# Two long fp32 dummy matmuls in place of the first bf16 ones, and a K pair split 2 to 6 around the second scale sums

## The chip, the cores and the metric

The kernel runs on one core of one Trainium2 chip. The metric is device time in microseconds (us) of one execution. The kernel before had a median of 244.20 us in three runs (244.18 to 244.32).

## The reference, cut to what matters

One block of a diffusion transformer: modulation from `c`, attention, MLP. Only its first lines touch this change.

```python
mod = (_silu(c) @ w_mod).reshape(B, 6, 1, D)              # B=2, D=1152
shift_a, scale_a, gate_a, shift_m, scale_m, gate_m = [mod[:, i] for i in range(6)]
h = _layernorm(x, axis=-1) * (1 + scale_a) + shift_a      # x: 2 x 256 x 1152
qkv = (h @ wqkv).reshape(B, N, 3, H, Dh)
# ... attention, output projection, second LayerNorm, MLP
```

## The kernel before: the parts that matter here

The program is a list of "units" per engine, and the waits follow from tracked reads and writes. TensorE takes its units in program order. Every instruction raises its engine's counter by one, and whoever depends on it waits for a value of that counter:

```python
for ins in u.instrs:
    ...
    bi = ins.fn(eng_handle)
    if ins.dma_sem is not None:
        bi.then_inc(dma_sems[ins.dma_sem], 16)
    else:
        bi.then_inc(sems[e], 1)
```

Some names. The "scale sums" are SiLU(c) times the scale columns of `w_mod`, made in matmuls only 2 columns wide (one per batch element). Their weights come in two sets of columns, each in three transfers ("pieces") of three row blocks. "K" is the K third of `qkv`, whose weights come one row block at a time. HBM is the chip's memory, from which the weights are loaded.

The start. Dummy matmuls are meant to bring TensorE to full clock before the needed work comes; their results are thrown away. (The code here is cut, and its comments are added.)

```python
# Pool: ones, identity (IDENT), ...
dve(270, lambda e: e.memset(Q4B, 0.0), [], [Q4B], "zq4b")
for i in range(5):
    S.unit("pe", 430.0, "warm_a%d" % i)
    mm(ps32(5), IDENT, Q4B, True, True)            # 128x512 bf16 dummy
# then c is transposed (c_T), and SiLU(c) is made on ScalarE and VectorE
# ...
warm(7, "b")                                       # seven more dummies
for n, behind in ((1, "bn_ln1_1_1"), (1, "aggr_ln1_1"), (2, "veps_ln1_1"), (2, "rstd_ln1_1")):
    warm(n, behind, behind)                        # dummies behind LayerNorm's steps
xn_T(1)                                            # first needed work: transposes
sca(0, 3)                                          # scale sums, first third of the weights
warm(1, "d")
sca(3, 6)                                          # second third
warm(1, "f", "aggr_ln1_2")
xn_T(0)
sca(6, 9)                                          # last third
xn_T(2, 0, 8)
# ...
k_first(0)                                         # first K matmuls
```

The second scale sums (the other five of nine column blocks, each `mod_kt` five matmuls 2 columns wide), with a K pair of eight 256-column matmuls around their last third:

```python
def k12(part):
    kts = ((range(3), ()), (range(3, KC), range(KC)))[part]     # KC = 4: 3 matmuls, then 5
    ...
for kt in range(KT):                               # KT = 9
    if kt == 6:
        k12(0)
    mod_kt(WSC, kt, 0, "scb_%d" % kt, (KC, KT))
hk(KC, 0)                                          # VectorE: first tile scaled by these sums
# ...
k12(1)
# then the K matmuls that read the scaled tiles
```

## Time and profile before

| | before |
|---|---|
| time, median of three | 244.20 us |
| span of the profiled run (243.62 us as a whole) | 242.3 us |
| TensorE busy | 238.4 us (98%) |
| needed work begins on TensorE | 7.98 us |
| first K matmul | 11.184 us |
| bubble at the second scale sums | 123 ns |

A row of the timeline has start, length, engine, line, what is written and read, the number of instructions, and in brackets how long the engine was idle before and what ended it. PEld is TensorE's weight load, which starts with its matmul or ahead of it, so its bracket shows what a matmul waited for. Beside what the views print, the trace holds a record of every rise of a semaphore: those of the transfers ("landings") and those of TensorE's counter. Numbers with three decimals here are from these records and from the start of each instruction.

### The profile page before, as it was taken

To read this page: it belongs to the slowest core of one execution; us is meant where nothing else is said; L and a number is where in the kernel's file an instruction comes from. 1 tells how busy PE (TensorE), PEld (TensorE's weight loads), DVE (VectorE), ACT (ScalarE), POOL (GpSimd) and SP (SyncE) were. 2 spreads that over 40 slices of the span, in tenths; PEclk is the share of its full clock that TensorE was granted. 3 is DMA by queue.
4 is the path that set the end of the run, shared out by engine and by line. 5 is a ranking of instruction groups with operands and counts; after the bars stand their busy time and mean duration, and the time that the engine had idled before them with its cause. 6 is when DMAs were issued, how large, how long until landed. Compare 5 with 4: busy or idle time off the path is not lost.

```text
span 242.3 us, 4076 instructions
## 1 busy us (share of the span) xinstructions
PE 238.4 (98%) x1763; PEld 147.5 (61%) x1763; DVE 120.3 (50%) x218; ACT 67.0 (28%) x136; POOL 21.2 (9%) x39
## 2 busy tenths in 40 slices
PE   7999999999999999999999999999999999999996
PEld 2698854556667666898444444444566656656676
DVE  3814388696997699789999500000022222111112
ACT  5820350355424107973233322222000000000000
POOL 1400000000021186400000000020000000000000
PEclk9999999999999999999999999999999999999999
DMA  6999999999996999989953498012000000000001
GB/s 241 330 381 392 391 392 391 397 413 405 391 356 196 351 395 391 391 266 394 314 164 82 150 320 313 0 29 72 0 16 19 16 16 19 16 16 16 19 24 27
DMA packets 30140, 51.59 MB, mean 213 GB/s; under 512 B 1703, under 2 KB 15787, under 8 KB 30123
## 3 DMA queue, kind: packets, MB, share of 16 engines
q1 hardware_dynamic: 29680, 50.14, 58.0%
q0 software_dynamic: 416, 1.19, 1.6%
q8 instruction: 14, 0.23, 0.4%
q14 instruction: 3, 0.02, 0.0%
q10 hardware_dynamic: 27, 0.00, 0.0%
HBM read 50.14 MB, written 1.19 MB: 212 GB/s over the span
## 4 chain that ended last, share of the span: by engine, by line
PE 97%; DVE 2%; POOL 0%; issue 0%; ACT 0%; DVEq 0%; POOLq 0%
PE psum L688 95%; PE psum L691 2%; DVE arena L739 1%; DVE arena L760 0%; POOL arena L711 0%; DVE arena L740 0%; DVE arena L1284 0%; DVE arena L1285 0%; POOL arena L710 0%; ACT arena L726 0%; DVE arena L727 0%; DVE arena L732 0%; DVE arena L742 0%; POOL arena L717 0%; POOL arena L715 0%
## 5 line engine op out<-in xcount | busy, mean ns | idle before, releaser
L688 PE MATMUL psum<-arena 128*128 128x384 bf16 (+10 forms) x1674 | 234.9, 306 | 1.6 <-POOL arena L711 1.5
L688 PEld LDWEIGHTS psum<-arena 128*128 128x128 bf16 (+3 forms) x1674 | 142.3, 97 | 90.0 <-issue 3.8
L1079 DVE SCALAR_TENSOR_TENSOR arena<-arena 128x1152 f32<-128x1152 bf16 x32 | 44.7, 1414 | 0.6
L1284 DVE TENSOR_TENSOR arena<-psum,arena 128x384 f32<-128x384 f32 (+3 forms) x14 | 7.0, 501 | 68.0 <-PE psum L688 68.0
L1193 ACT ACTIVATE arena<-psum 128x512 bf16<-128x512 f32 (+1 forms) x44 | 22.4, 520 | 42.7 <-PE psum L688 42.7
L683 ACT ACTIVATE arena<-psum 128x512 bf16<-128x512 f32 (+6 forms) x37 | 19.6, 549 | 39.5 <-PE psum L688 37.1
L685 DVE CAST arena<-psum 128x512 bf16<-128x512 f32 (+3 forms) x13 | 8.2, 641 | 11.4 <-PE psum L688 11.3
L669 POOL DMA_DIRECT2D dit_scratch<-arena x3 | 1.8, 616 | 115.7 <-DVE arena L685 58.9
L1161 POOL TENSOR_TENSOR arena<-arena 128x384 f32<-128x384 f32 x12 | 10.9, 910 | 10.8 <-DVE arena L1160 9.5
L1106 DVE CAST arena<-psum 72x32 bf16<-72x32 f32 x1 | 0.2, 186 | 21.3 <-PE psum L688 21.3
L739 DVE BATCH_NORM_STATS2 arena<-arena 128x6 f32<-128x384 f32 (+1 forms) x18 | 9.5, 552 | 0.1
L1166 ACT ACTIVATE arena<-arena 128x1152 bf16<-128x1152 f32 x4 | 5.3, 1345 | 11.9 <-DVE arena L1165 11.9
L691 PEld LDWEIGHTS psum<-arena 128*128 128x128 bf16 (+1 forms) x89 | 5.8, 98 | 2.5 <-issue 0.8
L1160 DVE TENSOR_TENSOR arena<-psum,arena 128x384 f32<-128x384 f32 x12 | 6.5, 549 | 1.6 <-DMA arena<-dit_scratch 1.6
L1285 DVE TENSOR_TENSOR arena<-arena 128x384 bf16<-128x384 f32 (+3 forms) x14 | 7.0, 501 | 0.5
L691 PE MATMUL psum<-arena 128*128 128x128 bf16 (+1 forms) x89 | 7.1, 219 | 0.1
L1180 DVE TENSOR_SCALAR arena<-psum,arena 128x128 bf16<-128x128 bf16 x20 | 5.4, 341 | 1.9 <-PE psum L691 1.9
L1183 ACT ACTIVATE arena<-psum,arena 128x128 bf16<-128x128 bf16 x16 | 6.0, 456 | 0.9 <-PE psum L688 0.6
L1086 DVE TENSOR_REDUCE arena<-arena 128x36 f32<-128x1152 f32 x4 | 5.4, 1348 | 0.0
L1083 DVE STREAM_TRANSPOSE arena<-arena 128x1152 f32<-128x1152 f32 x4 | 5.4, 1364 | 0.0
L1009 ACT ACTIVATE arena<-psum,arena 128x256 bf16<-128x256 f32 x8 | 3.7, 472 | 1.3 <-PE psum L688 0.9
L743 POOL TENSOR_TENSOR arena<-arena 128x1 f32<-128x1 f32 x6 | 3.6, 596 | 2.0 <-DVE arena L742 2.0
(48 smaller groups left out, 44.9 us busy)
## 6 DMA issues: line engine op xcount, KB each, us to landing
arena<-in_w_fc_dram SPq DMA_DIRECT2D x9, 1152.0 KB, 7.3
arena<-in_w_fc_dram SPq DMA_DIRECT2D x4, 2592.0 KB, 17.2
arena<-in_wqkv_dram SPq DMA_DIRECT2D x18, 288.0 KB, 10.2
arena<-in_w_mod_dram SPq DMA_DIRECT2D x3, 1728.0 KB, 20.2
arena<-in_w_mod_dram SPq DMA_DIRECT2D x3, 864.0 KB, 13.7
arena<-in_w_mod_dram SPq DMA_DIRECT2D x9, 288.0 KB, 10.5
arena<-in_wqkv_dram SPq DMA_DIRECT2D x1, 2592.0 KB, 16.6
arena<-in_wo_dram SPq DMA_DIRECT2D x1, 2592.0 KB, 24.4
```

The lines of the kernel that those rows point to most:

```text
L683: act(c_act(n), lambda e: e.activation(out=dst, in_=src, func=ACTF.Copy), [src], [dst], name)
L685: dve(c_dve_psum16(n) if psum16 else c_dve_psum32(n), lambda e: e.tensor_copy(dst, src), [src], [dst], name)
L688: S.instr(lambda e: e.matmul(o, lhsT=l, rhs=r, start=st, stop=sp, **kw), reads=[l, r], writes=[o])
L691: S.instr(lambda e: e.transpose(o, i_, idn), reads=[i_, idn], writes=[o])
L739: dve(550, lambda e, s=s, o=o: e.bn_stats(out=o, in_=s), [s], [o], "bn_%s_%d" % (tag, ci))
L1079: dve(1270, lambda e, w=w, s=s, acc=acc: e.scalar_tensor_tensor(out=acc, in0=w, scalar=s, in1=acc, op0=ALU.mult, op1=ALU.add), [w, s, acc] ...
L1160: dve(550, lambda e, o=o, ga=ga, x1c=x1c: e.tensor_tensor(out=x1c, in0=o, in1=ga, op=ALU.mult), [o, ga], [x1c], "wo_t1_%d_%d" % (t, ci))
L1161: S.op("pool", 930, lambda e, xs=xs, x1c=x1c: e.tensor_tensor(out=x1c, in0=x1c, in1=xs, op=ALU.add), reads=[x1c, xs], writes=[x1c], name=" ...
L1183: act(440, lambda e, o=o, dst=dst, s1=s1, s2=s2: e.activation(out=dst, in_=o, func=ACTF.Identity, scale=s1, bias=s2), [o, s1, s2], [dst], ...
L1193: act(c_act(ntok), lambda e: e.activation(out=dst, in_=o, func=ACTF.Gelu_apprx_tanh), [o], [dst], "gelu_%d_%d" % (f, tok0))
L1284: dve(c_dve_psum32(w), lambda e, o=o, gm=gm, t1=t1: e.tensor_tensor(out=t1, in0=o, in1=gm, op=ALU.mult), [o, gm], [t1], "fc2_t1_%d_%d" % ( ...
L1285: dve(c_dve_32(w), lambda e, t1=t1, x1c=x1c, ost=ost: e.tensor_tensor(out=ost, in0=t1, in1=x1c, op=ALU.add), [t1, x1c], [ost], "fc2_out_%d ...
```

## The change

Its intent: begin the dummies as soon as zeros are there, without the identity, and fill the time with a few long instructions (an fp32 matmul makes several passes); and let the last third of the second scale sums begin one K matmul sooner, so that VectorE gets them sooner and the bubble closes.

```diff
-        dve(270, lambda e: e.memset(Q4B, 0.0), [], [Q4B], "zq4b")
-        for i in range(5):
-            S.unit("pe", 430.0, "warm_a%d" % i)
-            mm(ps32(5), IDENT, Q4B, True, True)
+        ZF = sb(O_Q4B, 2048, F32)
+        dve(400, lambda e: e.memset(ZF, 0.0), [], [ZF], "zq4b")
+
+        def warm32(tag):
+            S.unit("pe", 1700.0, "warm32_%s" % tag)
+            mm(ps32(0), ZF[:, 0:P], ZF, True, True)
+
+        warm32("a")
+        S.unit("pe", 430.0, "warm_a")
+        mm(ps32(0), ZF[:, 0:64].bitcast(BF16), Q4B, True, True)
@@
-        warm(7, "b")
+        warm32("b")
+        warm(2, "b")
@@
-            kts = ((range(3), ()), (range(3, KC), range(KC)))[part]
+            kts = ((range(2), ()), (range(2, KC), range(KC)))[part]
```

## The prediction

> **What bounds the kernel now.** I read the page first: the busy shares, the slices, the chain that ended last. Then the waits of the first 14 us, because the change touches nothing later than 20 us, then the timelines of TensorE and VectorE there, and last the trace's own records of semaphore updates and of DMA landings.
>
> ```profile
> PE 238.4 (98%) x1763; PEld 147.5 (61%) x1763; DVE 120.3 (50%) x218; ACT 67.0 (28%) x136; POOL 21.2 (9%) x39
> ...
> PEclk9999999999999999999999999999999999999999
> DMA  6999999999996999989953498012000000000001
> ...
> PE 97%; DVE 2%; POOL 0%; issue 0%; ACT 0%; DVEq 0%; POOLq 0%
> ```
>
> TensorE is the bound: 97% of the chain, and busy in every slice. So only two things can move the end: an idle stretch of TensorE that goes away, or needed work on it that begins sooner. But "busy" includes dummy matmuls, so the first slices have to be opened.
>
> The next lines are the timeline of the start (start, length, engine, what it does; in brackets the idle time before and what ended it).
>
> ```profile
> 0.92 0.27 DVE L719 MEMSET arena<- 128x256 uint32 x1 [0.92 <-PEq L1346]
> ...
> 1.16 0.28 POOL L711 TENSOR_SCALAR_AFFINE_SELECT arena<-arena 128x128 bf16<-128x128 bf16 x1
> ...
> 1.50 2.31 PE L688 MATMUL psum<-arena 128*128 128x512 bf16 x5 [1.50 <-POOL arena L711]
> ...
> 7.97 0.51 PEld L691 LDWEIGHTS psum<-arena 128*128 128x128 bf16 x9 [0.64 <-DVE arena L760]
> ...
> 9.11 0.41 PEld L688 LDWEIGHTS psum<-arena 128*128 128x128 bf16 x13 [0.23 <-DMA arena<-in_w_mod_dram]
> ...
> 10.32 0.38 PEld L688 LDWEIGHTS psum<-arena 128*128 128x128 bf16 x12 [0.17 <-DMA arena<-in_w_mod_dram]
> ...
> 11.18 1.91 PE L688 MATMUL psum<-arena 128*128 128x256 bf16 x16
> ```
>
> The zeros are ready at 1.19 us (0.92 + 0.27), the identity at 1.44 (1.16 + 0.28), and the first dummy starts at 1.50: it is the identity that it waits for. From there to 7.97 us TensorE does nothing that the result needs except the small transpose of c at 3.74 us. The first needed work is the transposes at 7.97 us, behind the LayerNorm chain on VectorE. Then come the scale sums (128x2 matmuls), in three groups, and the second and third group each wait for a weight transfer. The landing records give the last piece of these two transfers at 9.066 and 10.280 us; TensorE goes on at 9.112 and 10.325. The first piece of the K weights lands at 11.048 us, and the first K matmul starts at 11.184. So three times in a row TensorE stood waiting for HBM: 84 ns, 164 ns and 83 ns beyond the normal spacing of the matmuls before. That start is bound by the transfers, not by the dummies.
>
> After 11.18 us TensorE runs on without a stop to about 19.4, and there is one bubble, at the second scale sums:
>
> ```profile
> 19.28 0.29 DVE L805 TENSOR_SCALAR arena<-arena,psum 128x256 bf16<-128x256 bf16 x1 [4.47 <-PE psum L688]
> 19.49 0.16 DVE L795 COPY arena<-psum 128x10 f32<-128x10 f32 x1
> 19.62 0.11 PEld L688 LDWEIGHTS psum<-arena 128*128 128x128 bf16 x2 [0.24 <-DVE arena L805]
> ```
>
> The last K matmul before it starts at 19.398 us and the next at 19.630, 232 ns where 109 is the spacing of 256-column matmuls: a bubble of 123 ns, ended by VectorE's first scaled tile (19.28 + 0.29 = 19.57). Later there is no other wait of this kind that the change reaches.
>
> **What the Trainium skill says.** "TensorE: Matmul & The Clock Gate", section "Part 1: The HAM clock gate", says that the array starts at half clock and is released after about 3.4 us of sustained activity. The trace agrees: 512-column dummies start 427 ns apart up to 4.749 us and 216 ns apart from 5.075; solving the one gap of 326 ns between them puts the change at 4.98 us, 3.48 us after the first dummy. The PEclk row does not show it.
>
> "FP8 and Floating Point Precision", section "TensorE Precision Notes", says that true fp32 takes four passes. The trace agrees with its own fp32 matmuls: each is two instructions, and of the 72-column one the second starts 62 ns after the first, two passes of 72 columns at 2.4 per ns. A row of the groups shows them:
>
> ```profile
> L688 PE MATMUL psum<-arena 128*128 128x72 f32 x2 | 0.3, 250 | 0.0
> ```
>
> "VectorE: DVE Perf Modes", section "Zero memsets can be issued as uint32 (trn2)", says that a memset takes one cycle per element whatever the type. At the 0.96 GHz that the page works with, 256 elements are 267 ns; the trace has 272. 512 fp32 elements should then take 533 + 5 = 538 ns (estimate), not the 400 in the diff.
>
> "TensorE: Matmul & The Clock Gate", section "The cost: per-tile semaphore tail", says that increments of a semaphore by matmuls serialize, about 26 ns each. The trace has the serializing with a larger number: 34.1 ns each wherever matmuls of 2 columns follow one another, which start every 26.7 ns. This decides the second part.
>
> **The change part by part.**
>
> (a) First dummies. Removed: five bf16 matmuls on the identity, 4 x 427 + 427 = 2.13 us from 1.50. Added: one fp32 matmul on zeros, four passes at half clock, 4 x 427 = 1.71 us, and one bf16 one, 0.43: 2.13 us again. Begun without the identity: the zeros' memset now ends at 0.915 + 0.538 = 1.453 us, where the identity was seen at 1.450 by its semaphore. So the start does not move: about 1.50, give or take 0.05. The saved wait is replaced by an equal one. With the fp32 weight load (190 ns a record against 97) the transpose of c may come up to 0.1 us later. That moves c's SiLU and the LayerNorm chain by as much.
>
> (b) What such a shift is worth. The LayerNorm chain meets TensorE at 7.98 us; after that TensorE has 84 ns of waiting for the transfer that lands at 9.066 and 164 ns for the one at 10.280. A chain later by up to 84 + 164 = 248 ns, or earlier by anything, gives the same 10.325. Sum of (a) and (b) on the path: 0.
>
> (c) Dummies behind the transpose of c: seven of 512 columns become one fp32 (four passes) and two bf16, so six passes, one fewer. They end about 0.2 us earlier, in front of a dummy that waits for VectorE anyway. Idle before 6.38 us grows from 0.23 to some 0.45. No needed work moves: 0. The clock has been released by then and this pause is short.
>
> (d) The K pair: three matmuls before the last three scale sums and five after become two and six. At first sight the scale sums start one matmul, 109 ns, sooner, and the bubble of 123 ns shrinks to 14. But VectorE does not start when the last small matmul is over. That one starts at 18.938 and ends in the records at 19.103; VectorE starts at 19.282. The semaphore records say why: from 17.618 us the counter of TensorE goes up every 34.1 ns without a pause until 19.292. Between the increment of the matmul before the scale sums (17.618) and the awaited one (19.258) lie 30 + 3 + 15 = 48 increments: 48 x 34.15 = 1.639, and 17.618 + 1.639 = 19.257. The three K matmuls in the middle are just long enough for the backlog to be nearly worked off (their last one ends at 18.726, its increment is at 18.745). With two there, 47 increments remain: 17.618 + 47 x 34.15 = 19.223. VectorE starts 34 ns earlier, not 109, and the first tile and the next K matmul with it: 19.596 in place of 19.630. TensorE's matmul count up to there is the same. Gain 0.034 us. The fifth K weight piece, landed at 19.347, does not stand in the way. Everything behind is bound by TensorE and moves along.
>
> Sum: 0 + 0 + 0 - 0.034, so 244.20 - 0.03 = 244.17 us.
>
> **The rivals.** One: the semaphore queue is not the limit, and the 109 ns are gained whole. For it: the diff's author chose this split, and the K matmuls are long enough that any rearrangement could let the counter catch up. Against it: 48 increments at an even 34 ns. Time 244.09.
>
> Two: the dummies really begin earlier, at about 1.36, if the longer memset takes the 400 ns of the diff. LayerNorm would come 0.1 us sooner, and the clock release too. Both are swallowed by the transfers at 9.07, 10.28 and 11.05 us: 244.15.
>
> Three: fp32 passes on zeros count less as activity for the clock gate, or the release falls one observation window later. By the skill's 3.4 us the release would then be at 8.4 us instead of 5.0, and 11.8 for two windows. At 8.4 some nine transposes run at half clock, 0.4 us more, of which 0.25 is absorbed by the waits: 244.4. At 11.8 the transposes, part of the scale sums and 0.6 us of K matmuls suffer: an estimate of +1 us, 245.2. Against it: the passes keep the array streaming, and the duration of the dummies is unchanged.
>
> Four: the kernel orders VectorE, ScalarE and GpSimd by a model of durations, and new durations could swap instructions later. Most orders near the start are fixed by name, and work off TensorE is mostly hidden, so I give this 0.2 us either way.
>
> **Range and chances.** The best guess is 244.2 (244.17). The three runs before span 0.14 us; another chip or another alignment of transfers may shift the whole by some tenths. The gains that I can imagine end at 0.2 us plus such a shift, the losses at 0.4 for one late clock window. I take 243.7 to 244.6. A change of 2% is 4.9 us, more than all first dummies and waits that are within its reach: faster 0.01, within 2% 0.98, slower 0.01.
>
> **What would show each step right or wrong.** (a) The memset row of the changed kernel should have 128x512 elements and about 538 ns, and the first matmul start at about 1.5 us; 400 ns and 1.36 would be rival two. The two fp32 records should start 853 ns apart at half clock. (b) The second and third group of scale sums should again wait for the weight transfer and start at 9.1 and 10.3, whatever the transposes at 8.0 do. (c) The 216 ns spacing should appear by 5 to 5.5 us; if matmuls of 128 columns at 8 us are 107 ns apart, rival three holds. (d) The first scaled tile should start some 34 ns earlier than 19.28 relative to the scale sums' begin, with 47 increments of 34 ns before it; 109 ns is rival one. The prediction is wrong as a whole if the end moves by more than half a microsecond with no shift of the transfers, or if groups later than 20 us change their order.

## The result, and the profile after

| | before | after |
|---|---|---|
| median | 244.32 us (6 runs, 244.18 to 244.87) | 244.42 us (6 runs, 244.01 to 244.95) |
| ratio of the fast runs | | 1.0001, 95% interval 0.9986 to 1.0017 |
| first K matmul, profiled run | 11.184 us | 11.678 us |
| from the first K matmul to the one after the bubble | 8.446 us | 8.415 us |
| last matmul starts | 239.899 us | 240.364 us |

A ratio is the mean time of one kernel's fast runs over that of the other's of the same rounds, so it is not quite the ratio of the medians quoted. The time is the same, and the 244.17 foreseen lies inside the spread of the runs.

From the page of the changed kernel, the busy shares and the chain that ended last:

```profile
PE 238.7 (98%) x1758; PEld 147.7 (61%) x1758; DVE 120.6 (50%) x218; ACT 67.1 (28%) x136; POOL 21.7 (9%) x39
...
PE 95%; DMA 3%; SPq 1%; DVE 0%; issue 0%
```

TensorE is the bound as before. But the first steps of the chain have changed their name: before, they led over VectorE (2%) to the identity; now 3% is a transfer. The next lines, from the timeline of the changed kernel's start, show where it joins:

```profile
0.97 0.48 DVE L720 MEMSET arena<- 128x512 f32 x1 [0.97 <-PEq L1353]
...
1.51 2.50 PE L688 MATMUL psum<-arena 128*128 128x512 f32 x3 [1.51 <-DVE arena L720]
...
3.94 0.10 PEld L691 LDWEIGHTS psum<-arena 18*128 18x128 bf16 x1 [1.26 <-DMA arena<-in_c_dram]
...
4.84 1.16 ACT L753 ACTIVATE arena<-arena 128x1152 bf16<-128x1152 bf16 x1 [0.48 <-DMA arena<-in_x_dram]
4.84 1.48 DVE L745 BATCH_NORM_STATS2 arena<-arena 128x6 f32<-128x384 bf16 x3
...
8.24 0.51 PEld L691 LDWEIGHTS psum<-arena 128*128 128x128 bf16 x9 [0.64 <-DVE arena L766]
...
9.42 0.41 PEld L688 LDWEIGHTS psum<-arena 128*128 128x128 bf16 x13 [0.27 <-DMA arena<-in_w_mod_dram]
...
10.82 0.38 PEld L688 LDWEIGHTS psum<-arena 128*128 128x128 bf16 x12 [0.36 <-DMA arena<-in_w_mod_dram]
...
11.68 0.49 PE L688 MATMUL psum<-arena 128*128 128x256 bf16 x3
```

The dummies wait for the longer memset now (start 1.51) instead of for the identity (1.50). The transpose of c comes 0.20 us later (3.94 against 3.74); its bracket names the transfer of c, but that had landed at 3.125, and it was the dummies in front that held it. The scale sums again wait for their weights, longer than before, because the transfers landed later: the third piece at 10.779 in place of 10.280 us, the first K weights at 11.542 in place of 11.048. The first K matmul is 0.136 us behind that landing in both profiles.

The bubble of the changed kernel, from the timeline there:

```profile
19.74 0.29 DVE L811 TENSOR_SCALAR arena<-arena,psum 128x256 bf16<-128x256 bf16 x1 [4.43 <-PE psum L688]
...
20.09 0.11 PEld L688 LDWEIGHTS psum<-arena 128*128 128x128 bf16 x2 [0.21 <-DVE arena L811]
```

It is 92 ns, was 123. The whole account of the two profiles: the first K matmul 0.494 us later, the stretch over the bubble 0.031 shorter, sum 0.463; the last matmul is 0.465 later. From the bubble to the last matmul both take 220.27 us. So the two profiles differ only before 12 us, and that by a landing. Whether the change caused the later landing is the first question for the experiments.

### The profile page after: what moved, and what is told of

The parts are those of the page before. It is cut to its first block, busy times and chain, and to the rows that moved or that the text cites. A ratio compares the mean times of both kernels' runs of the same rounds, so it can differ in the third digit from the quotient of the medians.

```text
span 242.7 us, 4066 instructions
## 1 busy us (share of the span) xinstructions
PE 238.7 (98%) x1758; PEld 147.7 (61%) x1758; DVE 120.6 (50%) x218; ACT 67.1 (28%) x136; POOL 21.7 (9%) x39
## 4 chain that ended last, share of the span: by engine, by line
PE 95%; DMA 3%; SPq 1%; DVE 0%; issue 0%
PE psum L688 93%; DMA arena<-in_w_mod_dram 3%; PE psum L691 2%; SPq L669 1%; DVE arena L1291 0%; DVE arena L1292 0%
## 5 line engine op out<-in xcount | busy, mean ns | idle before, releaser
L688 PE MATMUL psum<-arena 128*128 128x384 bf16 (+12 forms) x1669 | 235.3, 307 | 1.7 <-DVE arena L720 1.5
L688 PEld LDWEIGHTS psum<-arena 128*128 128x128 bf16 (+4 forms) x1669 | 142.5, 98 | 89.8 <-issue 4.0
L1168 POOL TENSOR_TENSOR arena<-arena 128x384 f32<-128x384 f32 x12 | 10.9, 912 | 11.1 <-DVE arena L1167 9.6
```

The lines of the kernel that those rows point to most:

```text
L688: S.instr(lambda e: e.matmul(o, lhsT=l, rhs=r, start=st, stop=sp, **kw), reads=[l, r], writes=[o])
L1168: S.op("pool", 930, lambda e, xs=xs, x1c=x1c: e.tensor_tensor(out=x1c, in0=x1c, in1=xs, op=ALU.add), reads=[x1c, xs], writes=[x1c], name=" ...
```

## The experiments

**The theory.** (1) The start is bound by whichever of two comes later: the landing of weights from HBM (first K matmul = landing of the first K weights + 0.136 us), or the LayerNorm chain (first K matmul = first transposes + 2.89 us). The dummies are beside both. Landings vary from execution to execution. (2) At the second scale sums VectorE waits for TensorE's counter, which goes up at most every 34 ns and lags behind the matmuls; one K matmul moved is worth one such step, not its 109 ns.

**The rivals.** The fp32 dummies delay the start themselves (by 0.2 us, by the clock, or by the transfers). And at the bubble, the last small matmul itself is awaited.

All kernels gave the right result except the two marked wrong. "Before" medians are of the same chip and rounds.

### Each part alone, and both kernels once more

Edit of `split_only`: only the last hunk of the diff.

> The K pair split 2 to 6, the dummies as before. Theory (increments of TensorE's counter queue at 34 ns each): in the trace VectorE's first scaled tile at the second scale sums starts 34 ns earlier relative to the first K matmul than in the kernel before, the bubble shrinks from 123 to about 89 ns, and the stretch from the first K matmul to the one after the bubble from 8.446 to 8.41 us. Rival (the last small matmul itself is awaited): 109 ns earlier, bubble 14 ns, stretch 8.34 us. Time: 0.03 us less by theory, 0.11 by the rival, neither to be told from zero by the clock alone.

Edit of `dummies_only`: the other hunks.

> The fp32 dummies alone, the split as before. Theory: time the same within 0.3 us; the transpose of c comes at 3.94 us, 0.2 later than before, because the first fp32 pass pair takes 1.01 us with its weight load in place of 0.85; the second and third group of scale sums still wait for their weight transfers, and the first K matmul follows the landing of the first K weights by 0.14 us. Stretch from the first K matmul to the one after the bubble 8.446 us as before. Rival (the fp32 dummies delay the real start by their 0.2 us): no wait for transfers in front of the scale sums, and 0.2 to 0.5 us slower.

`before_again` and `after_again` have no edit.

> The kernel before once more, for what varies by itself. Theory: the landing of the third scale piece and of the first K weights moves between executions by some tenths of a us (10.28 and 11.05 in its first profile, 10.78 and 11.54 in that of the changed kernel), and the first K matmul moves with it; so does the moment at which the dummies go over to full clock (4.97 in the first profile). Rival: both are properties of the kernel, and this run repeats 10.3, 11.0 and 5.0 within 0.1 us.

> The changed kernel once more. Theory: its first landings are drawn from the same spread as those of the kernel before, so they lie anywhere between 10.2 and 10.9 us (third scale piece), and the change to full clock between 5 and 8 us; the memset ends and the first dummy starts at 1.51 us again, and the transpose of c comes at 3.94. Rival (the fp32 dummies hold the clock or the transfers back): again 10.8 and 11.5, again 6.1 us for the clock.

Times: `split_only` 244.11 us, `dummies_only` 244.18, before 244.32; ratios 0.9993 (0.9980 to 1.0005) and 0.9995 (0.9981 to 1.0009), both the same. The single runs gave 244.29 (before) and 244.21 (after). So the clock separates nothing, as expected.

The traces do. The kernel before, run again, drew late landings (10.759 and 11.525 us), and its first K matmul came at 11.661, as in the first profile of the changed kernel. These are its weight loads in the timeline:

```profile
9.47 0.41 PEld L688 LDWEIGHTS psum<-arena 128*128 128x128 bf16 x13 [0.30 <-DMA arena<-in_w_mod_dram]
...
10.80 0.38 PEld L688 LDWEIGHTS psum<-arena 128*128 128x128 bf16 x12 [0.30 <-DMA arena<-in_w_mod_dram]
```

And `dummies_only` drew early ones (10.225 and 10.904), with the fp32 dummies in place. Its weight loads in the same stretch:

```profile
8.28 0.51 PEld L691 LDWEIGHTS psum<-arena 128*128 128x128 bf16 x9 [0.64 <-DVE arena L766]
8.74 0.98 PEld L688 LDWEIGHTS psum<-arena 128*128 128x128 bf16 x26
9.69 0.66 PEld L691 LDWEIGHTS psum<-arena 128*128 128x128 bf16 x9
10.31 0.42 PEld L688 LDWEIGHTS psum<-arena 128*128 128x128 bf16 x12
```

No bracket names a transfer: nothing waited. The first K matmul came at 11.172, which is the transposes (8.280) plus 2.892. This was a miss of a detail: I had expected waits for transfers here too, and the LayerNorm chain was the bound instead. It shows the second bound of the theory. And the half microsecond between the first two profiles does not need the change: the old dummies drew it too, and the fp32 ones did not draw it here. (The profile's chain of `dummies_only` leads from LayerNorm back over c to the dummies. But LayerNorm's first VectorE step began at 4.875 us, 24 ns behind the landing of x at 4.851, as in ten other profiles (23 to 25 ns); so x was the last to come.)

`dummies_only` also lost 79 ns in waits for ScalarE's copies and the second K weights just after 11.5 us, so its stretch from the first K matmul over the bubble is 8.549 us; the bubble itself was 120 ns. `after_again` lost 86 ns to the second K weights: stretch 8.496, bubble 93.

In `split_only` the stretch was 8.414 us (8.446 before; 8.41 expected by the queue, 8.34 by the rival). The bubble read 31 ns only because the scale sums themselves had waited 46 ns for their weights ahead of it. That accident is telling: sums that began 46 ns late did not make VectorE later, since the counter was behind anyway. Later, at 98.5 to 99.1 us, this execution alone lost another quarter of a microsecond waiting for VectorE's tiles of the second LayerNorm (220.56 us from the bubble to the last matmul, against 220.27); `after` and `after_again`, with the same split, did not.

The change to full clock came at 4.97 and 6.73 us in the two profiles of the kernel before, and at 6.13 and 4.87 in those of the changed one (4.87 is a little before the 5 to 8 expected). It varies by itself, and no first K matmul follows it.

### The queue of increments: three matmuls, two, none, and no queue

Edit of `split0`:

```diff
-    kts = ((range(3), ()), (range(3, KC), range(KC)))[part]
+    kts = ((range(0), ()), (range(0, KC), range(KC)))[part]
 ...
-            if kt == 6:
-                k12(0)
```

> The kernel before, with none of the pair's eight K matmuls ahead of the last three scale sums and all eight behind them. Theory (queue of increments, 34 ns each): three increments fewer lie before the awaited one, so VectorE's first scaled tile starts 0.103 us earlier relative to the first K matmul (7.995 us after it in place of 8.098), and the bubble falls to about 20 ns, the stretch from the first K matmul to the one after the bubble to 8.34 us. Rival (the last small matmul itself is awaited): 0.325 us earlier, 7.77 us after the first K matmul, bubble 0. A late landing of the third piece of the second scale columns could hold the sums up in both. Time: 0.1 us less, within the noise.

Edit of `one_inc`, on the kernel before:

```diff
+                    elif e == "pe":
+                        ins.eidx = eidx[e] + 1
+                        eidx[e] += ins is u.instrs[-1]
                     else:
                         eidx[e] += 1
 ...
-                    else:
+                    elif e != "pe" or ins is u.instrs[-1]:
                         bi.then_inc(sems[e], 1)
```

> The kernel before, with TensorE's counter raised once per group of matmuls (by its last one) in place of by every matmul. Theory: the queue of increments is gone, and VectorE starts some 45 ns after the end of the last small scale sum: 7.96 us after the first K matmul in place of 8.098; the bubble of 123 ns is below 15 ns and the stretch 8.33 us, with the split as it was. Rival (the queue is a symptom only and VectorE waits for something else): 8.098 and 123 ns again. Time: 0.1 to 0.2 us less, as the same queue stands at one or two later places.

`one_inc_after` is the same edit on the changed kernel.

> The changed kernel with TensorE's counter raised once per group. Theory: no bubble at the second scale sums (below 15 ns), VectorE's first scaled tile some 0.20 us after the start of the last small matmul in place of 0.42 in the changed kernel; with the split 2 to 6 there is nothing left for the split to win. Time 0.1 to 0.2 us below that of the kernel before, at the edge of what the clock can show.

Measured, from the starts in the traces:

| kernel | K matmuls ahead of the last third | VectorE's tile after the last small matmul | same, after the first K matmul | bubble |
|---|---|---|---|---|
| before | 3 | 0.344 us | 8.098 us | 123 ns |
| after | 2 | 0.420 | 8.064 | 92 |
| `split0` | 0 | 0.568 | 7.996 | 21 |
| `one_inc` | 3 | 0.203 | 8.110 (124 ns of it other waits) | 1 |
| `one_inc_after` | 2 | 0.204 | 7.844 | 1 |

Read the third column: the earlier the small matmuls begin, the longer VectorE waits after the last of them. Three K matmuls fewer end the small ones 0.326 us earlier, and VectorE starts only 0.102 us earlier, three increments of 34 ns. Take the increments away and the wait drops to 0.20 us with either split tried (three and two). The timeline of `one_inc` at this place:

```profile
18.80 1.16 PE L691 MATMUL psum<-arena 128*128 128x2 bf16 x16
...
19.21 0.29 DVE L808 TENSOR_SCALAR arena<-arena,psum 128x256 bf16<-128x256 bf16 x1 [4.33 <-PE psum L691]
```

and the one of `split0`:

```profile
19.71 1.17 PE L688 MATMUL psum<-arena 128*128 128x256 bf16 x9
...
20.26 0.29 DVE L805 TENSOR_SCALAR arena<-arena,psum 128x256 bf16<-128x256 bf16 x1 [4.37 <-PE psum L688]
20.32 0.70 SPq L669 DMA_DIRECT2D arena<-in_wqkv_dram  x1
20.46 0.17 DVE L795 COPY arena<-psum 128x10 f32<-128x10 f32 x1
```

In `one_inc` no weight load that waits for VectorE is left in the window; the matmuls run on. The 48 ns gap at 31.28 us of the kernel before is gone as well. From the place of the bubble to the last matmul it takes 220.20 us in place of 220.27.

The times: `split0` 244.14 us against 243.88 before, ratio 1.0007 (0.9993 to 1.0022); its profiled run drew the latest landings that no edit caused (first K matmul 12.260). `one_inc` 243.70 against 243.88, 0.9993 (0.9981 to 1.0006); `one_inc_after` 244.13 against 244.10, 0.9990 (0.9967 to 1.0012). The traces give `one_inc` 0.12 + 0.07 = 0.19 us, and the means agree in size, but the intervals hold 1. It is the best version by its traces; by the clock it is not shown to be faster.

### How many dummies: one, five, nine

Edits of `dummy1` and `dummy9`:

```diff
-        for i in range(5):
+        for i in range(1):        # dummy9: range(9)
```

> The kernel before, with one dummy in place of five ahead of the transpose of c, which then comes 1.4 us or more earlier (2.3 us). Theory: nothing is gained. The LayerNorm chain waits for the first x tile (landed at 4.3 to 4.9), and the first K matmul still follows the landing of the first K weights by 0.136 us or that of the third scale piece by 0.90. Time the same within 0.3 us. Rival (the start is bound by the dummies and c): the first K matmul 0.3 us or more before these landings allow, and a time 0.3 to 1.4 us shorter.

> The kernel before, with nine dummies ahead of the transpose of c. Theory: the transpose of c comes at 5.45 us or somewhat earlier if the clock is released within; the LayerNorm chain starts at 6.4, not at 4.6 to 4.9, and then it binds: transposes at about 9.7, first K matmul 2.9 us after them, at about 12.6, no waits for transfers in front of the scale sums, time 1.0 to 1.4 us longer. This is what a delay costs that exceeds the slack. Rival (dummies are hidden however many): first K matmul at 11.2 to 11.7, same time.

`dummy1`: the transpose of c at 2.278 us, 1.46 earlier, with x landed early too (4.126). The transposes came at 7.557, and TensorE then stood 328, 247 and 199 ns before the second and third piece and the first K weights:

```profile
7.55 0.51 PEld L691 LDWEIGHTS psum<-arena 128*128 128x128 bf16 x9 [0.64 <-DVE arena L760]
...
8.93 0.40 PEld L688 LDWEIGHTS psum<-arena 128*128 128x128 bf16 x13 [0.47 <-DMA arena<-in_w_mod_dram]
...
10.22 0.38 PEld L688 LDWEIGHTS psum<-arena 128*128 128x128 bf16 x12 [0.26 <-DMA arena<-in_w_mod_dram]
```

First K matmul 11.198, the landing at 11.063 plus 0.135. Time 244.04 against 243.88, ratio 1.0009 (0.9990 to 1.0027): the same.

`dummy9`: the transpose of c at 5.178 us, the transposes of x at 9.550, no wait for a transfer after them, first K matmul at 12.445 (2.895 behind the transposes). Time 245.19 against 243.88, ratio 1.0049 (1.0035 to 1.0063): by the ratio 1.2 us more, as expected (1.0 to 1.4).

```profile
9.55 0.51 PEld L691 LDWEIGHTS psum<-arena 128*128 128x128 bf16 x9 [0.50 <-DVE arena L760]
10.01 0.98 PEld L688 LDWEIGHTS psum<-arena 128*128 128x128 bf16 x26
10.96 0.66 PEld L691 LDWEIGHTS psum<-arena 128*128 128x128 bf16 x9
11.58 0.42 PEld L688 LDWEIGHTS psum<-arena 128*128 128x128 bf16 x12
```

Four dummies fewer are worth nothing, four more cost 1.2 us. That is slack seen from both sides, and the 0.2 us by which the fp32 dummies delay c lies inside it.

### More and fewer transfers

Edit of `extra_dma`:

```diff
             for k0, k1 in ((0, 3), (3, 6), (6, 9)):
+                if (ka, k0) == (0, 6):
+                    dma(WSM[:, 0:3, 0:KC * P], wmod_v[:, 0:3, 0:KC * P], 3 * P * KC * P * 2, "ld_extra", run=KC * P * 2)
```

> The kernel before, with one useless transfer of 384 KB put ahead of the third piece of the first scale columns. Theory (the start is bound by the transfers): that piece and the first K weights land later by what such a piece takes, 1.2 to 1.4 us; the first K matmul still follows the landing of the first K weights by 0.136 us, so it comes at 12.4 to 13.0, and the time grows by 1.2 to 1.4 us. Rival (the transfers are hidden behind LayerNorm and dummies): first K matmul at 11.2 to 11.7 us and the same time.

The third piece landed at 11.936 us, the first K weights at 12.692, and the first K matmul came at 12.828, 0.136 behind. TensorE stood 1.385 us for that piece:

```profile
9.88 0.70 PEld L691 LDWEIGHTS psum<-arena 128*128 128x128 bf16 x9
11.98 0.38 PEld L688 LDWEIGHTS psum<-arena 128*128 128x128 bf16 x12 [1.39 <-DMA arena<-in_w_mod_dram]
```

The trace is as expected, though from one execution: the third piece landed 0.55 us later than the latest without an added transfer (11.386, `split0`). The clock is less clear: 244.80 us against 244.10, ratio 1.0019 (0.9988 to 1.0050). Its four runs (244.47 to 245.49) lie mostly above those of before (243.59 to 244.54, and one of 245.60), but by about 0.7, not 1.2 to 1.4. The profiled run was the slowest of the four. With landings that vary by a microsecond in themselves four runs are too few for this, so the size stays open.

Edit of `less_dma` (wrong): the second and third piece are not loaded, and their matmuls use the first piece again. `less_dma_after` is the same on the changed kernel.

```diff
-            for k0, k1 in ((0, 3), (3, 6), (6, 9)):
+            for k0, k1 in ((0, 3), (3, 6), (6, 9)) if ka else ((0, 3),):
 ...
-                mm(ps32(7, ...), W[:, kt, f * 128:(f + 1) * 128], ...
+                mm(ps32(7, ...), W[:, kt % 3 if f < KC else kt, f * 128:(f + 1) * 128], ...
 ...
-            mm(ps32(1, 0, 2), WSC[:, kt, 0:P], ST[:, kt:18:9], ...
+            mm(ps32(1, 0, 2), WSC[:, kt % 3, 0:P], ST[:, kt:18:9], ...
```

> The kernel before, with the second and third piece of the first scale columns not loaded; their matmuls use the first piece again, so the result is wrong on purpose. Theory: the first K weights land some 2.4 us earlier, no wait for a transfer is left, and the LayerNorm chain takes over as the bound: the first K matmul comes 2.9 us after the first transposes, at 10.9 to 11.2 us. The gain is only what the transfers cost beyond that chain, 0.2 to 0.5 us of time. Rival (transfers alone are the bound): first K matmul near 9, time 2 us less.

> The same removal of two transfers, in the changed kernel (fp32 dummies, split 2 to 6); wrong result on purpose. Theory: the transpose of c 0.2 us later costs nothing even here as long as the first x tile lands at 4.78 us or later, as in most profiles, because LayerNorm waits for it; first K matmul again 2.9 us after the first transposes, 10.9 to 11.2, within 0.05 us of the other run for equal landings of x, and up to 0.2 us later only where x lands near 4.3. Rival (the dummies' 0.2 us reach the end once the transfers no longer cover them): first K matmul 0.2 us later than in the other run whatever the landing of x.

In `less_dma` the first K weights landed at 9.026 us, and still the first K matmul came at 10.999: 2.892 us behind the transposes (8.107), which were 3.430 us behind the landing of the first x tile (4.677). Its chain that ended last starts at that tile:

```profile
0.80 3.88 DMA arena<-in_x_dram
4.68 0.02 issue
4.70 1.49 DVE arena L739 x3
6.19 0.02 issue
6.22 0.25 DVE arena L740
```

Time 244.14 against 244.10, ratio 0.9996 (0.9970 to 1.0022). I had expected 0.2 to 0.5 us less, so this is a miss of the size: part was given back, 78 ns in waits for ScalarE's copies and the second K weights right after, and the rest is in the noise. Two transfers of three taken away gain nothing that the clock shows, because the LayerNorm chain stands right behind.

`less_dma_after`: 244.36 against 244.10, 1.0007 (0.9980 to 1.0033). This execution drew the latest x tile of all (5.097) and the latest change to full clock of all (7.83). The transposes came 3.527 us behind x, 0.1 more than elsewhere: the dummies in front of them still ran at 427 ns each, and the last of them was over late. The first K matmul came at 11.456 us, later than the 10.9 to 11.2 expected, because x was late: counted from the landing of x it is 6.359 us, against 6.322 in `less_dma`. That is 0.04 us where the rival asked 0.2. All profiles together say how much of the 0.2 can show. In nine profiles, of both kernels, the transposes follow the landing of x by 3.426 to 3.432 us, so x alone set them. In the first profile of before, where x landed at 4.334, they follow by 3.645, and in `one_inc_after`, with fp32 dummies and x at 4.714, by 3.462. Taking 3.43 off gives the moment at which c is out of VectorE's way: 4.55 us with the old dummies, 4.75 with the fp32 ones. In 12 of 14 profiles x landed at 4.67 us or later, so there the 0.2 us of the fp32 dummies are, or would be, hidden wholly, or but for 0.03 to 0.07 us. No profile with the fp32 dummies drew an early x (4.126 and 4.334 came with the old ones), so that case was not measured. By estimate the transfers cover it: 4.75 + 3.43 gives transposes at 8.18 and a first K matmul at 11.07 us, before the 11.184 and 11.198 that the landings allowed in those two profiles.

### All starts together

| kernel | landing of first K weights + 0.136 | first transposes + 2.892 | first K matmul |
|---|---|---|---|
| before | **11.184** | 10.871 | 11.184 |
| before again | **11.661** | 11.153 | 11.661 |
| after | **11.678** | 11.139 | 11.678 |
| after again | **11.581** | 11.123 | 11.580 |
| `split_only` | **11.284** | 11.129 | 11.283 |
| `dummies_only` | 11.040 | **11.172** | 11.172 |
| `dummy1` | **11.199** | 10.449 | 11.198 |
| `dummy9` | 10.955 | **12.442** | 12.445 |
| `extra_dma` | **12.828** | 11.154 | 12.828 |
| `less_dma` | 9.162 | **10.999** | 10.999 |

The constant 0.136 is that of the first profile of before, 2.892 that of `dummies_only`. The later of the two sums (bold) is the measured start within 3 ns in all ten (in these two profiles by construction). `split0` (12.261 and 12.260) and `one_inc_after` (11.361 and 11.361) fit as well; in `one_inc` and `less_dma_after`, bound by LayerNorm, the second sum is 0.06 us too long. The third piece and the first K weights land one after the other in every profile, so which of these two holds the start was not separated, save in `after_again`, where the third piece alone (10.535 us, plus the 0.90 of the first profile) would have allowed 11.44, and in `dummy1` (10.180, 11.08): there it was the K weights.

## Why the prediction was right, point by point

(a) "The start does not move: about 1.50": 1.51. The memset ended at 1.454 where 1.453 was foreseen, though its record reads 485 ns from a start 54 ns later, not 538. Its semaphore is the cleaner measure: 1.465 against 1.198 us, 267 ns for 256 elements more. "May come up to 0.1 us later" for the transpose of c was too small: 0.20. The term that was mis-sized seems to be the fp32 weight load, for 0.16 of the 0.20. From the start of the first pass pair to that of the second it took 1.013 us, not 0.853, and in that stretch lie both fp32 weight loads, of 287 and 333 ns in the records, where those of bf16 around them have at most 151. That they are the cause is argued from this; no run tested it. The rest is small: the later start, 0.014, and the first bf16 step, 0.399 us where 0.427 was counted.

(b) "The same 10.325" did not hold as a number: 10.827 in the first profile after. The step took the landings for fixed, and they are not. The transposes came 0.268 us later there, more than the 248 ns that the step allows, because x had landed 0.48 us later; it was luck for the sum that the weights came late as well. In the eleven profiles with all three pieces and no added transfer the third one landed between 10.07 and 11.39 us. That a wait for a transfer covers a shift of the chain in front of it held (the table, `dummy1`). The step missed a second cover, the landing of x in front of LayerNorm, which hides the later c in most executions.

(c) No cost: right, but the dummies did not end 0.2 us earlier. In `after_again`, where the clock was released about as early as in the first profile of before, they ended at 6.12 us against 6.16, since they began 0.20 later. And "the clock has been released by then" was not so in the first profile after: it came at 6.13 us, and no idle time was left at 6.38, because the dummies ran at half clock up to there. Over all profiles it fell between 4.70 and 7.83 us, with either kind of dummy. Only the two latest, 7.06 (`one_inc`) and 7.83 (`less_dma_after`), show a delay: the dummies ran on without a gap into the transposes, which came 0.06 and 0.10 us later behind x than elsewhere. The first K matmuls followed x by 6.319 and 6.359 us there, against 6.32 in `dummies_only` and `less_dma`, so at most 0.04 of it was left.

(d) 34 ns were foreseen, 31 measured (stretch 8.446 to 8.415; 8.098 to 8.064 for VectorE's tile, 34). The queue of 47 increments is what the records show: from 18.112 us, in steps of 34 ns, to 19.717. `split0` and `one_inc` confirm it against rival one. The clock could not have done so: 244.17 and rival one's 244.09 both lie inside the spread of the runs.

Of the other rivals: two (an earlier start) did not occur, the memset being as long as one cycle per element makes it. Three (a later clock) is not shown to come from the change: late releases were drawn with the old dummies too (6.73, 6.82 and 7.06 us), and its price was at most the 0.04 us of (c). Four did not occur: from the bubble to the last matmul both kernels take 220.27 us.

Two readings of the prediction were a little off, without effect on the sum. The change to full clock solves to 4.97 us, not 4.98. And before 7.97 us not only the transpose of c is needed: the two small matmuls at 3.865 and 3.913 write the 1 of (1 + scale).

What stays open: why the first landings differ by more than a microsecond between executions of the same program. No run here was made for it. In the two profiles with an early x (first `before`, `dummy1`) c had landed early too, at 2.21 and 2.23 us, against 3.04 to 3.21 in the other twelve. Nor do the landings alone make the spread of the runs: from the last matmul to the end of the span the profiles take 2.26 to 2.81 us, so the end varies by half a microsecond as well.

## What to carry to other kernels

Ask of a start which waits stand in series and which in parallel: an earlier end of the work in front of a wait is worth nothing as long as that wait ends later anyway, and the same slack lets a change be worse without being seen. When a consumer waits for a stream of tiny matmuls, look at the counter's records and not at the end of the last one; signalling once per group closed the bubble here (123 to 1 ns), though the clock did not show it. An effect of 0.03 us can be measured in a trace, between two marks that the noise does not reach, when the clock with its tenths cannot show it.

## What the Trainium skill lacked or had wrong

- "TensorE: Matmul & The Clock Gate", section "The cost: per-tile semaphore tail": it gives 26.3 ns per increment, 31.0 with what it adds per tile, and speaks of tiles packed into the array. Here each takes 34.1 ns, so an ordinary stream of 2-column matmuls, 26.7 ns apart, already falls behind: at the awaited increment the counter was 0.16 us late. The page's advice, one increment on the last, removed it.
- The same page, section "Part 1: The HAM clock gate": the transition is put at around 4 us of activity, give or take 0.5, and the window is called free-running. Here full clock came 3.2 to 6.3 us after the first dummy. That is more than the half microsecond, and is in keeping with what the section itself adds, that the number of slow matmuls differs from run to run.
- "FP8 and Floating Point Precision", section "TensorE Precision Notes": the four passes of fp32 are confirmed (853 ns per pass pair of 512 columns at half clock), but I found no time for the weight load of fp32 in particular on any page. The first pass pair of an fp32 matmul took 0.14 to 0.16 us more than the second here; in that stretch lie its weight loads, of 287 to 333 ns each.
- "VectorE: DVE Perf Modes", section "Zero memsets can be issued as uint32 (trn2)": nothing wrong. One cycle per element is confirmed by the semaphore (267 ns for 256 elements more), while the instruction's record, 485 ns for 512 elements and 272 for 256, would give 213.
- None of the pages that I read has the spread of the first transfers: the same 384 KB landed between 10.07 and 11.39 us after the start.
